# Pinned weight decodings, a sum of squares in two products, and one attention unit a step later

## The chip, the cores and the metric

The kernel runs on one core of a Trainium2 chip. The time is the device time of one execution in microseconds (us); the median of three runs before the change is 949.61 us (947.6 to 949.84). The core has four computing engines that matter here, each with its own instruction queue worked off in order: TensorE (PE; its weight loads are shown as PEld), VectorE (DVE), ScalarE (ACT) and GpSimd (POOL). SyncE (SP) issues the transfers. In an order or a timeline these short names stand.

## The reference

Three layers follow each other: a windowed attention with 32 global tokens per batch, a feed-forward layer with ELU, and a feed-forward layer with RMS normalisation and a SiLU gate. In short:

```python
x = attention(q_l, k_l, v_l, q_g, k_g, v_g)       # 4 batches, 8 heads, 512 + 32 rows, 64 wide
x = x.transpose(0, 2, 1, 3).reshape(2176, 512)    # 4 batches of 544 rows, 8 * 64 wide
h = x @ w_in                                      # 512 -> 2048
g = np.where(h > 0.0, h, np.exp(np.minimum(h, 0.0)) - 1.0)
x = g @ w_out                                     # 2048 -> 512
rms = np.sqrt(np.mean(x * x, axis=-1, keepdims=True) + 1e-06)
xn = x / rms * rms_g
g = xn @ w_gate                                   # 512 -> 1536
out = (g / (1.0 + np.exp(-g)) * (xn @ w_val)) @ w_out2  # 1536 -> 512
```

The weights arrive as 64-bit numbers; the rest as 32-bit.

## The kernel before, in words

**Number format.** Each 32-bit operand of the large products is kept as a high part and a low part in the reduced format fp32r, and a product is done in three passes (high by high, high by low, low by high; `PASSES`). Twelve such passes of 512 columns make one "first product" h (L128, 512 rows of weights deep) or one "second product" group y (L142).

**Weights.** A weight tile (two blocks of 128 rows by 512) is loaded as 64-bit words. Decoding it takes five steps and splitting two: ScalarE takes the absolute value of the upper word, read as a float (`dec_abs`, L79); VectorE clamps (L86), masks and shifts (L87) and merges in the bits of the two words (L88, L89); ScalarE casts the high part (L92); VectorE subtracts for the low part (L95). The feed-forward layer has 16 such tiles, numbered in the order `order1`: for each quarter G of the hidden width two tiles of w_in, then two of w_out. So tiles 0 and 1 are wanted from step 0 on, 2 from step 1 on, 8 and 9 by the first product of step 8, 12 and 13 by that of step 12.

**Stages.** A prologue computes the attention units 0 to 3 (a unit is 128 rows of one batch, all heads; units count from 0) and decodes tiles 0 to 2 in an order written by hand. Then four blocks of 512 rows follow (`moe_block`), each of 16 steps j. A step does the first product of step j (`mm1`), its activation (`act1`: on ScalarE L117, L118, on VectorE L119, then the split L135 on ScalarE and L136 on VectorE), and the second products of step j - 1 (`mm2`). During block b the attention units of the next batch are done in the gaps, one per four steps (`att_slot`): scores and exponentials at its first step (`a_S`, L211 to L221; `a_E`: maxima on VectorE L229, L230, eight exponentials on ScalarE L232), transposition at its second (`a_T`, L238, copied out by L240), value products and normalisation at its third (`a_PV`, L251; `a_N`, L264 to L266). In block 0 each step also ends with the decoding of one tile, 3 at step 0 to 15 at step 12 (`slot0`, `w1_decode`). The rest of the kernel (blocks 1 to 3, and the last layer in five groups of 512 or 384 rows, `prep` and the loop over k) uses the decoded weights; the last layer's weights are decoded during blocks 1 and 2, parked in HBM and fetched back through a small ring (`w2_fetch`). `prep` of a group has four parts: load, squares (L547, L553) added on GpSimd (L554), the sum over the 512 features by a product with a matrix of ones (L558) with root and reciprocal (L560, L561), and the scaled, split rows.

**What sets the order.** TensorE's order is the order of the code. On the other engines a scheduler moves instructions by its own estimate of when their inputs are there. Two things hold it: `tc.keep_in_program_order(ins)`, by which an instruction isn't moved ahead of the ones written before it, and `tc.issue_after(x)`, by which what is written inside comes after x. In block 0 the decodings stand under `issue_after` the last cast (`last[0]`, ScalarE) and the last subtraction (`last[1]`, VectorE) of the prologue's input.

Of the kernel before, what the change touches and what calls it, by code (L numbers as in the profile page):

```python
# [7 lines left out]
F32 = mybir.dt.float32  # L8
F32R = mybir.dt.float32r
# [3 lines left out]
ALU = mybir.AluOpType  # L13
# [17 lines left out]
def f(ap):  # L31
    return ap.bitcast(F32)
# [7 lines left out]
def fused_kernel(ctx: ExitStack, tc: tile.TileContext, kq, vl, gkq, gv, w_in, w_out, w_gate, w_val, w_o2, rms_g, consts, out):  # L40
# [36 lines left out]
    def dec_abs(pool, raw, keep=False):  # L77
        x = pool.tile([P, 1024], F32, tag="dx", name="dx")
        ins = nc.scalar.activation(x, f(words(raw)[:, :, 1]), AF.Abs)  # L79
        if keep:  # L80
            tc.keep_in_program_order(ins)
        return x
# [90 lines left out]
    with ExitStack() as ls:  # L173
# [107 lines left out]
        def att_slot(b, j, part):  # L281

            u, jj = 4 * (b + 1) + j // 4, j % 4
            if jj == 0 and part == 0:
                a_S(u, ATT2)
                a_E(u)
                load_kq(u + 1)
            if jj == 1 and part == 1:
                a_T(u, 0, aps, "att")
                a_T(u, 1, aps, "att")  # L290
            if jj == 2 and part == 0:
                a_PV(u, ATT2)
                a_N(u)
                load_v(u + 1)
# [55 lines left out]
        dxs, dsts = {}, {}  # L350

        def w1_abs(i):
            dxs[i] = dec_abs(dec["t"], raws[i])

        def w1_bits(i):
            dec_bits(dxs[i], raws.pop(i))
# [101 lines left out]
        def slot0(j, part, h):  # L458
            g = act1(h, 512, elu_a) if part == 0 else None
            att_slot(0, j, part)  # L460
            if part == 2:
                with tc.issue_after(last[0].ins), tc.issue_after(last[1].ins):
                    w1_decode()
                if j == 12:
                    w2_load()
                    w2_load()
            return g
# [24 lines left out]

    def second_start():
        bpools["bp"] = ctx.enter_context(tc.tile_pool(name="bp", bufs=1))
        bpools["ones"] = bpools["bp"].tile([P, P], F32, name="ones")
        nc.sync.dma_start(out=bpools["ones"], in_=consts[:, 4 * P:5 * P])
        bpools["gg"] = stage.enter_context(tc.tile_pool(name="ggp", bufs=2))
        bpools["st"] = stage.enter_context(tc.tile_pool(name="bst", bufs=4))
        prep(0, 0)
        w2_fetch()  # L500

    wraws, n_fetch = [], [0]

    def w2_fetch():
        while len(wraws) < 4 and n_fetch[0] < 18:
            raw = bpools["st"].tile([P, 1024], F32, tag="wraw", name="wraw")
            i = n_fetch[0]
            nc.sync.dma_start(out=raw.rearrange("p (a n) -> p a n", a=2), in_=wT[2 * i:2 * i + 2].rearrange("a p n -> p a n"))
            wraws.append(raw)
            n_fetch[0] += 1  # L510
# [24 lines left out]
    def prep(k, part):  # L535
        if k >= 5:
            return
        n = sizes[k] * P
        t0 = starts[k] * P
        if part == 0:  # L540
            y32 = moe.tile([P, 4, 512], F32, tag="x32", name="y32")
            nc.sync.dma_start(out=y32[:, :, :n], in_=yT[:, :, t0:t0 + n])
            y32_t[k] = y32
        elif part == 1:
            y32 = y32_t[k]
            acc = stg.tile([P, 512], F32, tag="stg", name="acc")
            nc.scalar.activation(acc[:, :n], y32[:, 0, :n], AF.Square)  # L547
            for c in range(1, 4):
                if k < 2:
                    sq = bpools["gg"].tile([P, 512], F32, tag="sq", name="sq")  # L550
                else:
                    sq = moe.tile([P, 512], F32, tag="e", name="sq", bufs=2)
                nc.scalar.activation(sq[:, :n], y32[:, c, :n], AF.Square)  # L553
                nc.gpsimd.tensor_tensor(out=acc[:, :n], in0=acc[:, :n], in1=sq[:, :n], op=ALU.add)  # L554
            acc_t[k] = acc
        elif part == 2:
            ms = hps.tile([P, 512], F32, tag="h", name="ms")
            nc.tensor.matmul(ms[:, :n], bpools["ones"], acc_t[k][:, :n], start=True, stop=True)  # L558
            rs = stg.tile([P, 512], F32, tag="stg", name="rs")
            nc.scalar.activation(rs[:, :n], ms[:, :n], AF.Sqrt, bias=eps, scale=1.0 / DM)  # L560
            nc.vector.reciprocal(rs[:, :n], rs[:, :n])  # L561
            rs_t[k] = rs
        else:
            y32, rs = y32_t[k], rs_t[k]
            if k % 2 == 0:
                xn = new_xT()
            else:
                xn = [bpools["xn"].tile([P, 2, 512], F32R, tag=f"xn{c}", name=f"xnB{c}") for c in range(4)]
            for c in range(4):
                nc.vector.scalar_tensor_tensor(out=y32[:, c, :n], in0=y32[:, c, :n], scalar=gcol[:, c:c + 1], in1=rs[:, :n], op0=ALU.mult, op1=ALU.mult)  # L570
                nc.scalar.copy(xn[c][:, 0, :n], y32[:, c, :n])
                nc.vector.tensor_tensor(out=xn[c][:, 1, :n], in0=y32[:, c, :n], in1=f(xn[c][:, 0, :n]), op=ALU.subtract)
            xn_t[k] = xn
# [337 lines left out]
```

## Time and profile before

| | us |
|---|---|
| median of 3 runs | 949.61 |
| the profiled execution | 949.2 |
| its span | 947.3 |
| TensorE busy | 915.8 (97%) |
| VectorE busy | 459.7 (49%) |
| ScalarE busy | 347.0 (37%) |
| GpSimd busy | 17.9 (2%) |

The share of a busy engine is a mean over the whole span: VectorE, at 49%, is busy without a gap in some stretches and nearly idle in others. In the page's 40 slices it stands at 9 in the third to fifth, which lie in block 0 of the first feed-forward layer; TensorE stands at 8 there and at 9 from the sixth on.

### The profile page before, as it was taken

What the parts mean: (1) busy time and instruction counts of PE and PEld (TensorE: products, weight loads), DVE (VectorE), ACT (ScalarE), POOL (GpSimd) and SP (SyncE); (2) the same over time, 40 slices, a digit from 0 to 9 for tenths busy, and PEclk for the clock granted to TensorE, in tenths of its full rate; (3) what the DMA queues carried; (4) which work ended last, traced back from release to release, by engine and by line L of the source; (5) the groups of instructions that cost most, each with busy time, mean ns of one, the idle gap of its engine ahead of it and who ended that gap; (6) DMA issues with size and microseconds to landing.
All of it is one profiled execution on the core that took longest, in us unless ns stands there. A gap on an engine that the chain in (4) does not pass through costs nothing.

```text
span 947.3 us, 15710 instructions
## 1 busy us (share of the span) xinstructions
PE 915.8 (97%) x6738; PEld 766.5 (81%) x6738; DVE 459.7 (49%) x791; ACT 347.0 (37%) x627; POOL 17.9 (2%) x19
## 2 busy tenths in 40 slices
PE   6788899999999999999999999999999999999997
PEld 5566688888887788777888888888889999999996
DVE  4799963666578874543786215221412241142111
ACT  4577544434443443332656213122312232232111
POOL 0000000000000000000100100001000100100000
PEclk9999999999999999999999999999999999999999
DMA  9675541544567763351644000100011010000000
GB/s 364 250 297 188 178 163 57 181 170 166 187 223 277 276 232 127 124 184 57 243 137 157 12 1 5 41 33 1 1 34 45 1 34 34 1 1 34 1 1 34
DMA packets 34445, 107.77 MB, mean 114 GB/s; under 512 B 3016, under 2 KB 5704, under 8 KB 31816
## 3 DMA queue, kind: packets, MB, share of 16 engines
q1 hardware_dynamic: 34376, 106.77, 31.5%
q8 instruction: 53, 0.87, 0.4%
q14 instruction: 16, 0.13, 0.0%
HBM read 88.41 MB, written 18.35 MB: 113 GB/s over the span
## 4 chain that ended last, share of the span: by engine, by line
PE 84%; DVE 8%; DMA 3%; issue 2%; ACT 2%; SPq 0%; ACTq 0%
PE y L142 15%; PE pg L633 15%; PE pv L633 15%; PE y L639 15%; PE h L128 14%; DVE dx L88 1%; DVE dx L89 1%; PE o L251 1%; PE yg L597 1%; PE s L221 1%; PE hg L581 1%; PE ptp L238 1%; DMA kq<-in_kq 1%; PE s L216 1%; DVE wA L95 1%
## 5 line engine op out<-in xcount | busy, mean ns | idle before, releaser
L142 PE MATMUL y<-g,wA 128*128 128x512 f32 x768 | 198.8, 402 | 6.1 <-DVE g L136 5.7
L128 PE MATMUL h<-xT,wA 128*128 128x512 f32 x768 | 186.8, 392 | 1.3 <-DVE xT L276 1.3
L142 PEld LDWEIGHTS y<-g,wA 128*128 128x128 f32 x768 | 140.2, 189 | 40.9 <-DVE g L136 8.4
L128 PEld LDWEIGHTS h<-xT,wA 128*128 128x128 f32 x768 | 144.2, 189 | 32.3 <-DVE xT L276 1.5
L806 DVE TENSOR_TENSOR silu<-pv,silu 128x384 f32<-128x384 f32 (+1 forms) x60 | 36.7, 611 | 257.2 <-PE pv L633 249.1
L639 PE MATMUL y<-wB,p 128*128 128x512 f32 x612 | 149.0, 391 | 0.0
L639 PEld LDWEIGHTS y<-wB,p 128*128 128x128 f32 x612 | 114.4, 188 | 22.3
L805 ACT ACTIVATE silu<-pg 128x384 f32<-128x384 f32 (+1 forms) x60 | 32.1, 534 | 158.9 <-PE pg L633 158.7
L633 PE MATMUL pv<-xT,wB 128*128 128x384 f32 (+1 forms) x432 | 88.4, 352 | 0.0
L633 PEld LDWEIGHTS pv<-xT,wB 128*128 128x128 f32 x432 | 77.3, 188 | 5.6
L808 ACT CAST p<-silu 128x384 fp32r<-128x384 f32 (+1 forms) x60 | 33.3, 555 | 127.0 <-DVE silu L806 126.8
L135 ACT CAST g<-e 128x512 fp32r<-128x512 f32 x64 | 39.8, 622 | 75.8 <-DVE e L111 71.0
L633 PE MATMUL pv<-xnB,wB 128*128 128x512 f32 (+1 forms) x288 | 61.5, 362 | 0.0
L109 ACT ACTIVATE e<-h 128x512 f32<-128x512 f32 x48 | 28.9, 601 | 85.3 <-PE h L128 77.9
L633 PE MATMUL pg<-xT,wB 128*128 128x384 f32 (+1 forms) x288 | 60.1, 357 | 0.0
L633 PEld LDWEIGHTS pg<-xT,wB 128*128 128x128 f32 x288 | 52.1, 188 | 5.8 <-issue 0.5
L633 PEld LDWEIGHTS pv<-xnB,wB 128*128 128x128 f32 x288 | 52.2, 188 | 5.6
L809 DVE TENSOR_TENSOR p<-silu,p 128x384 fp32r<-128x384 f32 (+1 forms) x60 | 38.0, 634 | 35.5 <-ACT p L808 35.5
L110 DVE TENSOR_SCALAR e<-e 128x512 f32<-128x512 f32 x52 | 22.2, 428 | 65.2 <-ACT e L109 65.0
L136 DVE TENSOR_TENSOR g<-e,g 128x512 fp32r<-128x512 f32 x64 | 45.1, 705 | 17.6 <-ACT g L135 16.3
L79 ACT ACTIVATE dx<-raw 128x1024 f32<-128x1024 f32 x34 | 39.5, 1162 | 10.9 <-DMA raw<-in_moe_w_out 4.3
L232 ACT ACTIVATE E<-s,mx 128x128 f32<-128x128 f32 x128 | 35.1, 384 | 22.3 <-DVE mx L230 22.3
(179 smaller groups left out, 948.5 us busy)
## 6 DMA issues: line engine op xcount, KB each, us to landing
raw<-in_moe_w_out SPq DMA_DIRECT2D x14, 1024.0 KB, 6.1
wT<-dx SPq DMA_DIRECT2D x18, 512.0 KB, 3.4
wraw<-wT SPq DMA_DIRECT2D x18, 512.0 KB, 4.2
raw<-in_moe_w_in SPq DMA_DIRECT2D x8, 1024.0 KB, 7.2
raw<-in_moe_w_gate SPq DMA_DIRECT2D x6, 1024.0 KB, 6.2
raw<-in_moe_w_val SPq DMA_DIRECT2D x6, 1024.0 KB, 6.8
gvr<-in_gv SPq DMA_DIRECT2D x8, 640.0 KB, 4.6
gkq<-in_gkq SPq DMA_DIRECT2D x4, 1152.0 KB, 5.2
```

What stands on the lines that cost most here:

```text
L79: ins = nc.scalar.activation(x, f(words(raw)[:, :, 1]), AF.Abs)
L128: nc.tensor.matmul(h[:, :n], W1[c, G][:, ws, o:o + P], xT[c][:, xs, :n], start=(k == 0), stop=(k == 11))
L135: nc.scalar.copy(g[:, 0, :n], e[:, :n])
L136: nc.vector.tensor_tensor(out=g[:, 1, :n], in0=e[:, :n], in1=f(g[:, 0, :n]), op=ALU.subtract)
L142: nc.tensor.matmul(ys[dc][:, :n], W2[j][:, ws, dc * P:(dc + 1) * P], g[:, gs, :n], start=(j == 0 and k == 0), stop=(j == 15 and k == 2))
L232: nc.scalar.activation(e[par][:, pr, :], ss[par][:, pr, :], AF.Exp, bias=mx[:, par, pr:pr + 1], scale=SCALE)
L633: nc.tensor.matmul(ps[:, :n], W[c, G3][:, ws, o:o + P], xn[c][:, xs, :n], start=(k == 0), stop=(k == 11))
L639: nc.tensor.matmul(os_[t], p[:, pp, t * P:(t + 1) * P], Wo[j][:, ww, :], start=(j == 0 and k == 0), stop=(j == 11 and k == 2))
L805: nc.scalar.activation(s[:, :n], pg[:, :n], AF.Silu)
L806: nc.vector.tensor_tensor(out=s[:, :n], in0=pv[:, :n], in1=s[:, :n], op=ALU.mult)
L808: nc.scalar.copy(p[:, 0, :n], s[:, :n])
L809: nc.vector.tensor_tensor(out=p[:, 1, :n], in0=s[:, :n], in1=f(p[:, 0, :n]), op=ALU.subtract)
```

## The change

It has three parts. In block 0 the absolute values of tiles 3 and up carry `keep`, so ScalarE's order has them where the code has them, at the end of a step; they no longer come after the prologue's last cast explicitly, only after the last subtraction. Unit 4, the fifth, has its scores, transposition and value products one step later (steps 1, 2 and 3 in place of 0, 1 and 2). In the last layer, the sums of squares are split into a high and a low part, and the product with ones is done twice in fp32r in place of once in 32 bits; the ones are written by GpSimd in place of being loaded, and the ring of fetched weights has three places in place of four, which makes the room.

```diff
@@ att_slot
             u, jj = 4 * (b + 1) + j // 4, j % 4
+            if b == 0 and j < 4:
+
+                jj = j - 1
             if jj == 0 and part == 0:
                 a_S(u, ATT2)
@@ w1_abs
-            dxs[i] = dec_abs(dec["t"], raws[i])
+            dxs[i] = dec_abs(dec["t"], raws[i], keep=i > 2)
@@ slot0
             if part == 2:
-                with tc.issue_after(last[0].ins), tc.issue_after(last[1].ins):
+                with tc.issue_after(last[1].ins):
                     w1_decode()
@@ second_start
-        bpools["ones"] = bpools["bp"].tile([P, P], F32, name="ones")
-        nc.sync.dma_start(out=bpools["ones"], in_=consts[:, 4 * P:5 * P])
+        bpools["ones"] = bpools["bp"].tile([P, P], F32R, name="ones")
+        nc.gpsimd.memset(f(bpools["ones"]), 1.0)
...
-        bpools["st"] = stage.enter_context(tc.tile_pool(name="bst", bufs=4))
+        bpools["st"] = stage.enter_context(tc.tile_pool(name="bst", bufs=3))
@@ w2_fetch
-        while len(wraws) < 4 and n_fetch[0] < 18:
+        while len(wraws) < 3 and n_fetch[0] < 18:
@@ prep, part 1
-            acc_t[k] = acc
+            a2 = bpools["bp"].tile([P, 2, 512], F32R, tag="a2", name="a2")
+            nc.scalar.copy(a2[:, 0, :n], acc[:, :n])
+            nc.vector.tensor_tensor(out=a2[:, 1, :n], in0=acc[:, :n], in1=f(a2[:, 0, :n]), op=ALU.subtract)
+            acc_t[k] = a2
@@ prep, part 2
-            nc.tensor.matmul(ms[:, :n], bpools["ones"], acc_t[k][:, :n], start=True, stop=True)
+            acc = acc_t[k]
+            for i in range(2):
+                nc.tensor.matmul(ms[:, :n], bpools["ones"], acc[:, i, :n], start=(i == 0), stop=(i == 1))
```

ScalarE, first steps of block 0, from the input's last cast on. Before (dx is the absolute value of a tile, wA its high part, E the exponentials of unit 4):

```order
L79 ACTIVATE dx<-raw 128x1024
L117 ACTIVATE e<-h 128x512
L118 ACTIVATE e<-e 128x512
L92 CAST wA<-dx 128x2x512
L135 CAST g<-e 128x512
L92 CAST wA<-dx 128x2x512
L117 ACTIVATE e<-h 128x512
L118 ACTIVATE e<-e 128x512
L79 ACTIVATE dx<-raw 128x1024
L232 ACTIVATE E<-s,mx 128x128 x8
L135 CAST g<-e 128x512
```

The same place after the change:

```order
L117 ACTIVATE e<-h 128x512
L118 ACTIVATE e<-e 128x512
L92 CAST wA<-dx 128x2x512
L135 CAST g<-e 128x512
L79 ACTIVATE dx<-raw 128x1024
L117 ACTIVATE e<-h 128x512
L118 ACTIVATE e<-e 128x512
L135 CAST g<-e 128x512
L92 CAST wA<-dx 128x2x512
L232 ACTIVATE E<-s,mx 128x128 x8
L79 ACTIVATE dx<-raw 128x1024
L117 ACTIVATE e<-h 128x512
```

The absolute value of tile 3 moved from ahead of step 0's activation to behind it, that of tile 4 from ahead of the exponentials to behind them, and the high part of tile 3 from between the steps to behind step 1's activation.

ScalarE, around the exponentials of unit 5 (step 4). Before; the two absolute values are those of tiles 8 and 9:

```order
L79 ACTIVATE dx<-raw 128x1024
L92 CAST wA<-dx 128x2x512
L135 CAST g<-e 128x512
L79 ACTIVATE dx<-raw 128x1024
L232 ACTIVATE E<-s,mx 128x128 x8
L92 CAST wA<-dx 128x2x512
L117 ACTIVATE e<-h 128x512
```

After the change; the absolute values are those of tiles 7 and 8:

```order
L135 CAST g<-e 128x512
L232 ACTIVATE E<-s,mx 128x128 x8
L79 ACTIVATE dx<-raw 128x1024
L117 ACTIVATE e<-h 128x512
L118 ACTIVATE e<-e 128x512
L92 CAST wA<-dx 128x2x512
L240 COPY ET<-ptp 128x512
L135 CAST g<-e 128x512
L240 COPY ET<-ptp 128x512
L79 ACTIVATE dx<-raw 128x1024
```

Two absolute values stood ahead of the exponentials; now the next one, of an earlier tile, stands behind them.

VectorE, from the second maximum of unit 5 on. Before (tiles 8 and 9 are under way):

```order
L230 TENSOR_SCALAR mx<-mx 128x4
L87 TENSOR_SCALAR dx<-dx 128x1024
L89 SCALAR_TENSOR_TENSOR dx<-raw,dx 128x1024
L88 SCALAR_TENSOR_TENSOR dx<-raw,dx 128x1024
L95 TENSOR_TENSOR wA<-dx,wA 128x2x512
L89 SCALAR_TENSOR_TENSOR dx<-raw,dx 128x1024
L119 SCALAR_TENSOR_TENSOR e<-e,h 128x512
```

After the change (tile 7 follows, alone):

```order
L230 TENSOR_SCALAR mx<-mx 128x4 x2
L86 TENSOR_SCALAR dx<-dx 128x1024
L87 TENSOR_SCALAR dx<-dx 128x1024
L88 SCALAR_TENSOR_TENSOR dx<-raw,dx 128x1024
L89 SCALAR_TENSOR_TENSOR dx<-raw,dx 128x1024
L119 SCALAR_TENSOR_TENSOR e<-e,h 128x512
L95 TENSOR_TENSOR wA<-dx,wA 128x2x512
```

Two tiles were interleaved there; now one tile's steps follow each other, and the first of them is the one that needs the absolute value behind the exponentials.

## Rows read from the trace of the kernel before

**Rows 1.** The page: the span, and TensorE's busy time, share, instructions.

```profile
span 947.3 us, 15710 instructions
...
PE 915.8 (97%) x6738; PEld 766.5 (81%) x6738; DVE 459.7 (49%) x791; ACT 347.0 (37%) x627; POOL 17.9 (2%) x19
```

**Rows 2.** Waits of TensorE, 42 to 165 us: total, times, longest.

```profile
PE y L142 <- DVE g L136: 5.3, 4, 2.5
```

**Rows 3.** Busy time by stretch: us, PE, PEld, DVE, ACT, POOL, clock, DMA.

```profile
42.60:119.50 76.90, 67.94 (x623) 53.41 (x624) 76.66 (x107) 50.77 (x83) 0.00 (x0) 0.98 0.57 207
54.50:57.90 3.40, 3.40 (x13) 2.51 (x12) 3.33 (x6) 3.40 (x10) 0.00 (x0) 0.50 1.02 423
```

**Rows 4.** Timeline of TensorE, block 0: start, us, engine, line, what.

```profile
42.63 3.01 PE L128 MATMUL h<-xT,wA 128*128 128x512 f32 x12 [1.29 <-DVE xT L276]
...
45.48 0.61 PE L211 MATMUL s<-masks,identr 128*128 128x512 f32 x2
...
47.97 3.00 PE L128 MATMUL h<-xT,wA 128*128 128x512 f32 x12
...
102.95 2.88 PE L128 MATMUL h<-xT,wA 128*128 128x512 f32 x12
...
134.02 2.88 PE L128 MATMUL h<-xT,wA 128*128 128x512 f32 x12
...
146.15 1.03 PE L238 MATMUL ptp<-ident,E 128*128 128x128 f32 x8
...
151.21 1.12 PE L251 MATMUL o<-v__1454,ET 128*32 128x65 f32 x64
...
162.33 2.88 PE L128 MATMUL h<-xT,wA 128*128 128x512 f32 x12
```

**Rows 5.** Timeline of VectorE, block 0.

```profile
56.16 0.69 DVE L87 TENSOR_SCALAR dx<-dx 128x1024 int32<-128x1024 int32 x1
56.89 1.23 DVE L88 SCALAR_TENSOR_TENSOR dx<-raw,dx 128x1024 int32<-128x1024 int32 x1
58.03 0.69 DVE L136 TENSOR_TENSOR g<-e,g 128x512 fp32r<-128x512 f32 x1
58.64 0.69 DVE L86 TENSOR_SCALAR dx<-dx 128x1024 f32<-128x1024 f32 x1
...
90.89 1.22 DVE L95 TENSOR_TENSOR wA<-dx,wA 128x1024 fp32r<-128x1024 f32 x1
...
116.02 1.22 DVE L95 TENSOR_TENSOR wA<-dx,wA 128x1024 fp32r<-128x1024 f32 x1
```

**Rows 6.** Timeline of ScalarE, block 0.

```profile
54.13 2.16 ACT L232 ACTIVATE E<-s,mx 128x128 f32<-128x128 f32 x8
...
79.58 1.15 ACT L79 ACTIVATE dx<-raw 128x1024 f32<-128x1024 f32 x1 [0.78 <-DVE wA L95]
```

**Rows 7.** Timeline of TensorE, last layer, around two sums of squares.

```profile
573.56 2.88 PE L633 MATMUL pv<-xT,wB 128*128 128x512 f32 x12
576.28 2.88 PE L639 MATMUL y<-wB,p 128*128 128x512 f32 x12
...
582.63 0.62 PE L633 MATMUL pv<-xT,wB 128*128 128x512 f32 x2
...
753.56 2.24 PE L639 MATMUL y<-wB,p 128*128 128x512 f32 x9
...
757.75 2.24 PE L633 MATMUL pv<-xT,wB 128*128 128x384 f32 x12
759.83 2.24 PE L639 MATMUL y<-wB,p 128*128 128x512 f32 x9
...
764.64 1.55 PE L633 MATMUL pv<-xT,wB 128*128 128x384 f32 x8
```

**Rows 8.** Timeline of ScalarE and GpSimd after the fifth group's squares.

```profile
827.44 0.49 ACT L805 ACTIVATE silu<-pg 128x384 f32<-128x384 f32 x1 [1.99 <-PE pg L633]
...
825.53 1.01 POOL L554 TENSOR_TENSOR acc<-acc,sq 128x384 f32<-128x384 f32 x1 [0.64 <-ACT sq L553]
```

## The prediction

> **What bounds the kernel now.** I read the page first: TensorE is busy for 97% of the span [rows 1]. So only what shortens its work, or a wait of its own, can show. The waits of TensorE, asked for the first block of the mixture (42 to 165 us), come second: its largest is for the activated tile g, 5.3 us in four waits, the longest 2.5 [rows 2]. After that block TensorE waits for nearly nothing until the output is stored. Third, the busy time of each engine by stretch: from 42.6 to 119.5 us VectorE works 76.66 of 76.90 us [rows 3]. In that block it, not TensorE, is the engine without slack: it must decode and split twelve weight tiles (2 to 13; 14 and 15 follow) beside the activations. The timelines then give the price of each instruction and the four marks that I use, the starts of the block's first products of steps 0, 8, 12 and, for the next block, 16: 42.63, 102.95, 134.02 and 162.33 us [rows 4].
>
> **The pinned decodings and the later scores.** Price on VectorE, from one start to the next [rows 5]: the two clamps and masks of a tile 0.60 us each (0.73 when the next one needs the result, that is 0.12 more), the two bit merges and the low part 1.13 each, so 4.59 us for a tile; the two instructions of an activated tile 0.60 each. An attention unit adds some 2.35 (two reductions at 0.60, eight small ones). Four steps with four tiles and one unit make 4 x 4.59 + 4 x 1.20 + 2.35 = 25.5 us, and the trace agrees: the low parts of tiles 9 and 13 start 25.1 us apart [rows 5].
>
> In the old order ScalarE takes the absolute value of tile 9 at 79.58 us, ahead of the exponentials of unit 5 [rows 6], and the tile is split at 92.1 us, over 12 us before step 8 multiplies by its second half. That lead keeps VectorE fed. The second and third of the pieces in the section on the change show what the pin does: behind the unit's eight exponentials now stands the absolute value of tile 7, not two tiles ahead of them. I laid both orders out by hand, each instruction at the later of its engine being free and its inputs being there, with the durations of these rows. For the old order that gives 119.2 us from mark 0 to mark 16, where the trace has 119.7, so the method is good to about 0.5 us. For the new order:
>
> - Steps 0 and 1 gain. The scores of unit 4 (units count from 0) no longer stand between the first two products, tile 3 is no longer interleaved with tile 2, and the longest wait for g [rows 2] goes.
> - What is late next is step 2's own g. ScalarE's high part of tile 3 stands in front of the exponentials and of step 2's activation and waits 3.6 us for VectorE; TensorE then waits 4.6 us ahead of step 2's second products. At step 4 the two orders are level within 0.4 us.
> - VectorE now idles, where it was full. After the maxima of unit 5 it waits for eight exponentials (2.0 to 2.2 us [rows 6]) and then the absolute value (1.15 us): 3.2 us. Up to tile 9 I count seven more such gaps of 0.6 to 1.9 us, all behind a pinned absolute value or a high part queued on ScalarE: 10.2 us in all. Its work to that point is 8 tiles x 4.59 + 16 x 0.60 + 2 units x 2.35 + the first 1.2 of tile 10 = 52.2 us, and some 14 results needed at once cost 14 x 0.12 = 1.7. So tile 9 is split at 43.1 + 52.2 + 10.2 + 1.7 = 107.2 us.
> - TensorE wants it after 8.5 first products and 7 second ones of 2.72 us, two scores of 2.49 (45.48 to 47.97), two sets of transposes and two value products (1.03 and 1.12 each in the rows, of which some 0.15 lies under the next: 3.7 together) and 8.8 us of laid-out waits: 42.6 + 42.2 + 5.0 + 3.7 + 8.8 = 102.3 us [rows 4]. It stands 4.9 us. The old order passes this point at 102.95 + 1.36 = 104.3, so the new one is 2.9 us late.
> - The next four steps repeat it. VectorE needs 25.5 + 9 x 0.12 + gaps of 3.2, 0.6, 0.8 and 0.6 = 31.8 us against 31.07 between the marks [rows 4]: tile 13 holds step 12 for another 4.8 us, and the delay is 3.6.
> - From there the old order needs 26.95 us to mark 16, the new one 26.4 of work and 1.8 of waits (step 14's value products wait for a copy queued behind tile 15's high part on ScalarE): 1.2 more. Delay at the end of the block: 4.8 us. Nothing behind the block gives it back, since TensorE is busy without a gap there.
>
> **The clock.** After the 2.5 us wait the granted clock is 0.50 (1.2 of 2.4 GHz) from 54.5 to 57.9 us [rows 3], and once more late in the block; the half clock costs TensorE up to 3.4 / 2 = 1.7 us each time. The new order has three waits of about 4.8 us (steps 2, 8, 12), longer than those. I take one fall more than before, and two thirds of its price since VectorE is the late one after some of them: 1.1 us. Bounds: 0 and 3 x 1.7 = 5.1.
>
> **The sum of squares.** Per unit of the last stage the 32-bit product stands between two groups. From the second products to the next value products TensorE takes 582.63 - 576.28 = 6.35 us with it and 5.44 without (two groups of 2.72, as 573.56 to 576.28): 0.91 us. For 384 columns it is 4.81 against 4.19: 0.62 [rows 7]. Two full-rate products are 2 x 0.227 and 2 x 0.18. The gain is 2 x 0.46 + 3 x 0.26 = 1.7 us, and TensorE has no slack there, so all of it counts. The nearest rows bound it: nothing if a product of the new form took 0.48 us like a half of the old one, 1.7 if it runs like its neighbours; I take 1.7. The two added splits per unit are hidden: the third sum on GpSimd ends at 826.54, the cast of 0.5 us is done by 827.1, and ScalarE waits for pg until 827.44 in any case [rows 8]. Without that cover each would cost at most the 1.0 us by which it would hold ScalarE, five times. Fetch buffers (three for four), the ones written by GpSimd instead of a transfer and the fewer transfers on SyncE I set at nothing, between -0.5 and +1.0 together: no product of that stage waits for its weights. The raw load of tile 11 now queues behind a value load on SyncE until step 5 has multiplied; it lands some 18 us ahead of its use in my layout.
>
> **Sum.** 4.8 + 1.1 - 1.7 = +4.2 us. The profiled execution took 949.2 us (span 947.3), 0.4 below the median of 949.61; on the median the change gives 953.8 us.
>
> A rule that would make the first stall larger: the Trainium skill, VectorE: DVE Perf Modes, "The DRAIN you can't avoid", says that a Vector instruction starts only once the pipe of the one before it is empty, whatever the semaphores. By it the step between bit merges would be their 1.23 us, and tile 9 would come some 4 us later still. The row has the next one 0.09 us before that end (56.89 + 1.23 against 58.03 [rows 5]), so I use 1.13.
>
> **The rivals.**
> - *The clock falls after each of the three long waits and TensorE is then the late engine.* Place: steps 2, 8 and 12. Price 5.1 in place of 1.1: 949.6 + 8.2 = 957.8 us. For it: the fall at 54.5 followed a wait of half that length. Against: where VectorE is late anyway, a slow TensorE costs nothing; after the first fall the old order lost little. The Trainium skill, TensorE: Matmul & The Clock Gate, "HAM oscillation — how this bites in real kernels", has idle gaps between groups of products lower the clock, which is this rival; the stretch at 0.50 agrees.
> - *The pins work as worded.* The activations of the first steps come sooner, and tiles 9 and 13 are there in time. It decides if VectorE's gaps stay under some 5 us up to tile 9. Then four fifths of the 5.3 us [rows 2] go, with the 1.7 of the squares: 949.6 - 4.2 - 1.7 = 943.7, faster. For it: the longest wait does go. Against: the 3.2 us behind the exponentials, which no other work on VectorE's order fills.
> - *It cancels out.* The stalls at tiles 9 and 13 are real but half as long (a gap or two filled earlier than I laid it), 1.5 to 2 us, and the squares pay for them: 949.6 us.
> - *The split of the squares does not gain*, because the cast waits for GpSimd and holds the Silu behind it: then 955.5. The covers above speak against it; it lies in the range.
>
> **How the numbers follow.** Under 0.3%, 2.8 us here, a measurement can't tell a change from none. Forecast 0.64, with its own range 951.5 to 956.5; of it 0.06 lies within 0.3%. Clock rival 0.14. Cancelling out 0.15. Faster rival 0.07. So slower 0.58 + 0.14 = 0.72, same 0.15 + 0.06 = 0.21, faster 0.07. The range 948.5 to 957.5 leaves out most of the faster rival (0.06), half of the clock one (0.07) and little else.
>
> **What would show it.** Right: two new waits of TensorE of about 4.8 us inside the first products of steps 8 and 12, put down to the low part of a weight tile on VectorE; idle time of VectorE for the absolute value, 3.2 us after each unit's maxima; the last low part of the block near 155 us instead of 128; 0.45 us instead of 0.91 for each sum of squares. Wrong: first products of steps 8 and 12 without a wait, mark 16 less than 2 us later than 119.7 after mark 0, or a new wait in the last stage.

## The result, and the profile after

The changed kernel takes 956.68 us (median of 4 runs, 955.62 to 959.74) against 949.12 (median of 4, 947.6 to 949.84). The ratio is 1.0087, with a 95% interval of 1.0058 to 1.0116: slower by 7.6 us, where 4.2 on top of the median of 949.61, 953.8 us in all, was forecast. The profiled execution took 957.72 us. The page answers [rows 1]: the span is 8.6 us longer, and TensorE is busy 2.7 us longer for the same number of instructions.

```profile
span 955.9 us, 15715 instructions
...
PE 918.5 (96%) x6738; PEld 770.4 (81%) x6738; DVE 466.4 (49%) x796; ACT 348.7 (36%) x632; POOL 18.6 (2%) x20
```

The waits of TensorE in the first block, 42 to 172 us (total, times, longest), answer [rows 2]. The wait for g has shrunk from 5.3 us to 2.4 and 1.8; in its place stand 6.7 and 1.4 us for a weight tile, wA.

```profile
PE h L128 <- ACT wA L92: 6.7, 2, 3.4
PE y L142 <- DVE g L136: 2.4, 1, 2.4
PE y L142 <- ACT g L135: 1.8, 1, 1.8
PE h L128 <- DVE wA L95: 1.4, 2, 0.9
```

TensorE's timeline (start, us, line, what, idle time before it and its releaser) answers [rows 4] and shows the places: in front of the second products of step 2's g (which stand in step 3), and inside the first products of steps 8 and 12.

```profile
67.76 0.50 PE L142 MATMUL y<-g,wA 128*128 128x512 f32 x1 [1.76 <-ACT g L135]
70.61 4.86 PE L142 MATMUL y<-g,wA 128*128 128x512 f32 x11 [2.36 <-DVE g L136]
...
102.47 1.52 PE L128 MATMUL h<-xT,wA 128*128 128x512 f32 x6
107.33 0.73 PE L128 MATMUL h<-xT,wA 128*128 128x512 f32 x2 [3.34 <-ACT wA L92]
108.99 1.90 PE L128 MATMUL h<-xT,wA 128*128 128x512 f32 x4 [0.93 <-DVE wA L95]
...
135.37 1.52 PE L128 MATMUL h<-xT,wA 128*128 128x512 f32 x6
140.24 1.22 PE L128 MATMUL h<-xT,wA 128*128 128x512 f32 x2 [3.35 <-ACT wA L92]
141.90 2.08 PE L128 MATMUL h<-xT,wA 128*128 128x512 f32 x4 [0.44 <-DVE wA L95]
```

The busy time by stretch (us; then PE, PEld, DVE, ACT, POOL; granted clock; DMA) answers [rows 3]: first the whole block (mark 0 is 43.65, mark 16, the first product of the next block, 170.96), then the three stretches at or near half clock, each behind one of those waits. The second fence has the same block of the kernel before and the second fall of its clock, which [rows 3] do not show.

```profile
43.65:170.96 127.31, 114.14 (x1005) 90.13 (x1005) 100.36 (x147) 69.81 (x119) 0.00 (x0) 0.93 0.46 164
68.30:75.10 6.80, 4.49 (x11) 3.52 (x12) 6.80 (x12) 2.19 (x2) 0.00 (x0) 0.50 1.01 415
109.20:112.80 3.60, 3.60 (x70) 2.54 (x69) 2.67 (x3) 1.84 (x3) 0.00 (x0) 0.53 0.07 15
139.97:146.80 6.83, 6.12 (x78) 4.09 (x80) 5.45 (x7) 2.90 (x5) 0.00 (x0) 0.50 0.57 192
```

```profile
42.63:162.33 119.70, 110.78 (x1004) 88.48 (x1005) 97.62 (x147) 70.82 (x119) 0.00 (x0) 0.97 0.49 175
119.30:122.70 3.40, 3.40 (x9) 2.65 (x9) 2.96 (x5) 3.14 (x5) 0.00 (x0) 0.51 0.52 142
```

The block is 127.31 - 119.70 = 7.61 us longer: 114.14 - 110.78 = 3.36 of it is TensorE working longer on the same products, and the other 4.25 is TensorE standing. The 3.36 is clock: half of the work at half clock is 7.1 us in this block (4.49, 3.60 and 6.12 us) and 3.4 in the block before (twice 3.40). The split says what TensorE did, not what either part would have cost without the other. On VectorE (answer to [rows 5]) the eight exponentials and the absolute value leave 3.19 us empty behind unit 5's maxima; the low part of tile 9 starts at 107.71 (before at 90.89), that of the block's last tile at 157.71 (before at 128.20). On ScalarE ([rows 6]) the absolute value stands where the order shown ahead of the prediction puts it.

```profile
83.34 0.29 DVE L230 TENSOR_SCALAR mx<-mx 128x4 f32<-128x4 f32 x2
86.81 0.70 DVE L86 TENSOR_SCALAR dx<-dx 128x1024 f32<-128x1024 f32 x1 [3.19 <-ACT dx L79]
...
107.71 1.22 DVE L95 TENSOR_TENSOR wA<-dx,wA 128x1024 fp32r<-128x1024 f32 x1
...
157.71 1.23 DVE L95 TENSOR_TENSOR wA<-dx,wA 128x1024 fp32r<-128x1024 f32 x1 [1.12 <-ACT wA L92]
```

```profile
83.59 2.18 ACT L232 ACTIVATE E<-s,mx 128x128 f32<-128x128 f32 x8 [2.09 <-PE y L142]
85.61 1.17 ACT L79 ACTIVATE dx<-raw 128x1024 f32<-128x1024 f32 x1
```

In the last layer (TensorE, answer to [rows 7]) a sum of squares now costs 589.44 - 588.99 = 0.45 us at 512 columns and 771.46 - 771.11 = 0.35 at 384. On ScalarE and GpSimd (answer to [rows 8]) the fifth group's cast is over at 836.01, and the Silu waits for pg as before.

```profile
588.99 0.62 PE L566 MATMUL ms<-a,ones 128*128 128x512 f32 x2
589.44 2.88 PE L641 MATMUL pg<-xT,wB 128*128 128x512 f32 x12
```

```profile
835.50 0.51 ACT L559 CAST a<-acc 128x384 fp32r<-128x384 f32 x1 [1.12 <-POOL acc L557]
836.36 0.49 ACT L813 ACTIVATE silu<-pg 128x384 f32<-128x384 f32 x1 [0.35 <-PE pg L641]
```

Three marks on TensorE split the rest: mark 16, the first gx, a transposition of the gathered rows (403.88 us before, 413.75 after), and the end of the last product (940.70 and 949.34).

| stretch | before | after | difference |
|---|---|---|---|
| span's start to mark 0 | 42.63 | 43.65 | +1.02 |
| block 0 (mark 0 to 16) | 119.70 | 127.31 | +7.61 |
| mark 16 to first gx | 241.55 | 242.79 | +1.24 |
| first gx to last product | 536.82 | 535.59 | -1.23 |
| rest of the span | 6.60 | 6.56 | -0.04 |

The first line differs from execution to execution: in the profiles of the other kernels below mark 0 lies between 41.87 and 43.69, with the same instructions of TensorE and VectorE in front of it. The other four sum to 7.58 us, near the 7.56 between the two medians. One of the twelve executions of the kernel below that keeps tile 3's place only took 3183.74 us; the ratio leaves it out.

### The profile page after: what moved, and what is told of

It is laid out like the page before. It is cut to its first block, busy times and chain, and to the rows that moved or that the text cites. A ratio compares the mean times of both kernels' runs of the same rounds, so it can differ in the third digit from the quotient of the medians.

```text
span 955.9 us, 15715 instructions
## 1 busy us (share of the span) xinstructions
PE 918.5 (96%) x6738; PEld 770.4 (81%) x6738; DVE 466.4 (49%) x796; ACT 348.7 (36%) x632; POOL 18.6 (2%) x20
## 4 chain that ended last, share of the span: by engine, by line
PE 80%; DVE 10%; ACT 5%; DMA 2%; issue 2%; SPq 0%; ACTq 0%; DVEq 0%
PE pg L641 15%; PE pv L641 15%; PE y L647 15%; PE y L142 14%; PE h L128 13%; DVE dx L88 2%; DVE dx L89 2%; PE o L251 1%; DMA kq<-in_kq 1%; PE s L221 1%; ACT E L232 1%; DVE g L136 1%; PE s L216 1%; PE ptp L238 1%; DVE dx L86 1%
## 5 line engine op out<-in xcount | busy, mean ns | idle before, releaser
L88 DVE SCALAR_TENSOR_TENSOR dx<-raw,dx 128x1024 int32<-128x1024 int32 x34 | 42.1, 1239 | 0.9
```

The lines of the kernel that those rows point to most:

```text
L88: nc.vector.scalar_tensor_tensor(out=i32(x), in0=word[:, :, 1], scalar=-0x40000000, in1=i32(x), op0=ALU.bitwise_and, op1=ALU.bitwise_or)
```

## The experiments

All kernels below were timed in five rounds; the kernel before had medians of 948.71, 948.70 and 948.85 us beside the three sets of four. "Block 0" is mark 0 to mark 16 of the profiled execution.

### Which edit costs

Theory A was the prediction's: the kept places starve VectorE. B was that the later scores do the harm, C that the squares do. The edits, in this order: `keep` alone; the later scores alone; the squares alone; and the changed kernel without `keep`.

```diff
# e_pin: the kernel before, with
+            dxs[i] = dec_abs(dec["t"], raws[i], keep=i > 2)
# e_shift: the kernel before, with
+            if b == 0 and j < 4:
+                jj = j - 1
# e_squares: the kernel before, with the new prep part 1 and 2, ones by memset, ring of three
# e_nopin: the changed kernel, with
-            dxs[i] = dec_abs(dec["t"], raws[i], keep=i > 2)
+            dxs[i] = dec_abs(dec["t"], raws[i])
```

> The kernel before with one of the three edits alone: absolute values of weight tiles 3 to 15 kept at their place in ScalarE's order; no later scores, old squares. Theory A (the kept places starve VectorE of weight tiles, TensorE then waits for a low part, and its clock falls behind the waits): +3.5 us from the waits by a hand lay-out of the new order, and 0 to 5 more from the clock, so 953 to 958, with two new waits inside first products of the first block put down to a low part of a weight tile. Theory B (the later scores of unit 4 cause the loss, since they put exponentials in front of tile work): within 1 us of before, no such waits. Theory C (the new squares cost more than they save): within 1 us of before.

> The kernel before with the later scores alone: unit 4's scores, transposes and value products one step later in the first block, no kept places, old squares. Theory A: no loss, -0.5 us by the lay-out (-2 to +1), no wait for a weight tile in the first block. Theory B: +4 to +8 us, with the wait in front of the second products of step 2 and the clock fall behind it as in the changed kernel. Theory C: within 1 us of before.

> The kernel before with the squares alone: high and low part of the accumulated squares multiplied by ones at the full rate, ones written on chip, three buffers for the second half's weights instead of four. The first block stays as it was. Theory A: -1.7 us (0.46 saved twice and 0.26 three times by the rows of the two kernels), 946.9 to 948.3. Theory C: the added copy and subtraction, or the ring of three, cost more than the 1.7 us: 0 to +3 us, with new TensorE waits after 480 us. Theory B says nothing here.

> The changed kernel with the kept places alone taken out again: later scores and new squares stay. Theory A: faster than before, -1 to -4 us by the lay-out (the later scores and the squares both gain), the waits for low parts of weight tiles gone from the first block. Theory B: still +4 to +6 us, the wait in front of step 2's second products still there. Theory C: still slower than before by +2 or more, the loss behind 480 us.

| kernel | median, us | ratio to before, 95% | block 0 |
|---|---|---|---|
| kept places alone | 955.50 | 1.0070 [1.0055, 1.0085] | 125.57 |
| later scores alone | 949.45 | 1.0005 [0.9996, 1.0014] | 119.39 |
| squares alone | 947.89 | 0.9989 [0.9977, 1.0000] | 120.36 |
| changed, without kept places | 948.55 | 0.9993 [0.9982, 1.0005] | 119.47 |

The kept places alone bring 6.8 of the 7.6 us, and without them nothing is left of the loss. B and C fall. The order behind the prologue's last cast, which the change drops, costs nothing that shows: the last kernel drops it too, and its order in block 0 is that of the kernel with the later scores alone; only one absolute value stands elsewhere, just ahead of mark 0. The two waits for wA are there in the first kernel (its waits of TensorE, first fence) and its granted clock over the block is 0.92 (second fence, by stretch); in the other three they are absent.

```profile
PE h L128 <- ACT wA L92: 4.6, 2, 3.2
```

```profile
43.69:169.26 125.57, 114.87 (x1004) 91.52 (x1005) 99.83 (x147) 70.03 (x119) 0.00 (x0) 0.92 0.47 167
```

A's gain for the kernel without kept places (-1 to -4) was a miss: -0.2 us, within the measurement. Its block 0 gains 0.23, its last layer 1.46 us, and 0.64 goes at the start of block 2, by a wait that is taken up below. The squares alone were to bring 1.7 and bring 0.8. Their profile shows where a part goes: ScalarE waits 2.99 us for a fetched weight tile in front of the first root, the reciprocal behind it starts late, VectorE then works without a gap, and a transposition on TensorE waits 0.82 us for it (ScalarE's and TensorE's timelines).

```profile
486.08 1.05 ACT L92 CAST wB<-wraw 128x1024 fp32r<-128x1024 f32 x1 [2.99 <-DMA wraw<-wT]
```

```profile
500.59 0.63 PE L593 MATMUL egt<-ident,e 128*128 128x128 f32 x4 [0.82 <-DVE e L111]
```

### Is it the place behind the exponentials?

If VectorE starves because the kept absolute value stands behind a unit's exponentials, it is enough to issue it a step earlier, with every place still kept. One kernel does that, one keeps tile 3's place only.

```diff
# e_abs_early: the changed kernel, with
-                w1_abs(i)
+                if i not in dxs:
+                    w1_abs(i)
...
                 w1_load()
+                if i + 1 < 16:
+                    w1_abs(i + 1)
# e_pin_to3: the changed kernel, with keep=2 < i <= 3
```

> The changed kernel with one thing moved: the absolute value of the next weight tile is issued at the end of the step before, so that on ScalarE it stands ahead of a unit's eight exponentials instead of behind them; all places stay kept. Theory A (VectorE starves because the kept absolute value stands behind the exponentials): VectorE's idle stretches of 2 to 3 us behind a unit's maxima go, the waits for a low part inside steps 8 and 12 go, and block 0 is no longer than before's 119.7 us; the lay-out makes it 112 to 114, so 942 to 949 us in all. Theory D (a kept order as such costs, wherever the absolute value stands, since ScalarE can no longer pick what is ready): still 953 to 957 us, with waits of the same size elsewhere.

> The changed kernel with one kept place only, that of weight tile 3 in step 0; tiles 4 to 15 float. Theory A (what costs is the kept place behind a unit's exponentials, and tile 3 has none ahead of it): no loss, 945.5 to 949 us, no wait for a low part at steps 8 and 12, block 0 within 119.7 -2.5 to +0.5. Theory D (any kept place costs in proportion to their number): a tenth of the loss, within 1 us of the kernel without kept places, 948.5. If tile 3's place alone shifts the whole chain late: +2 us or more.

Measured: 941.62 us, ratio 0.9922 [0.9909, 0.9935], for the first, 947.24 us, ratio 0.9981 [0.9968, 0.9994], for the second. D falls, A stands. In the first kernel ScalarE takes the absolute value at 77.56, ahead of the exponentials at 79.67 (first fence), and VectorE goes from unit 5's maxima to the next tile without a gap (second fence), where the changed kernel had 3.19 us. Block 0 is 113.48 us, at a granted clock of 1.00 (third fence).

```profile
77.56 1.13 ACT L79 ACTIVATE dx<-raw 128x1024 f32<-128x1024 f32 x1
79.67 2.18 ACT L232 ACTIVATE E<-s,mx 128x128 f32<-128x128 f32 x8 [0.98 <-DVE mx L230]
```

```profile
79.41 0.23 DVE L230 TENSOR_SCALAR mx<-mx 128x4 f32<-128x4 f32 x2
79.55 0.69 DVE L86 TENSOR_SCALAR dx<-dx 128x1024 f32<-128x1024 f32 x1
```

```profile
42.38:155.86 113.48, 107.75 (x1005) 86.12 (x1006) 100.10 (x147) 70.39 (x119) 0.00 (x0) 1.00 0.51 184
```

That is 7.1 us faster than the kernel before. Two more kernels asked which edits this gain needs: the same without the later scores (and with the old squares), and the same with the places free.

```diff
# e_early_noshift: e_pin, with the absolute value one step ahead
# e_early_float: e_abs_early, without keep
```

> The kernel before with kept places and the absolute value one step ahead, but without the later scores of unit 4 and with the old squares. If the earlier absolute value alone makes the gain of 7 us: 941.5 to 944 us. If it only undoes what the kept places cost (the lay-out: block 0 +0.1 to +0.5) and the gain needs the later scores as well: 948 to 950 us, 5 to 7 below the kernel with kept places alone.

> The kernel that was 7 us faster, without the kept places: the absolute value of the next tile is written one step ahead, but its place on ScalarE is left to the scheduler. If the kept place is what holds it ahead of the exponentials (theory A): the gain goes for the most part, 946 to 949 us, near the changed kernel without kept places. If writing it earlier is enough: 941 to 943 us.

Measured: 951.89 us, 1.0035 [1.0021, 1.0048], and 947.84 us, 0.9989 [0.9980, 0.9998]. So the gain needs all three: kept, early, and the later scores (the old squares of the first kernel are worth 2.0 us at most, by the stretches below). In the second kernel the order of ScalarE and VectorE in block 0 is, instruction by instruction, that of the changed kernel without kept places: where the scheduler was free, it undid the earlier writing. The first kernel gains 3.6 us over the kept places alone, less than the 5 to 7 expected, and stays slower than before. Its rows show the same fault at another place. Without the later scores unit 4's exponentials fall into step 0 and stand ahead of even the early absolute value (ScalarE); VectorE waits 3.19 us for it, and TensorE 4.21 us for a tile at step 4.

```profile
51.28 2.17 ACT L232 ACTIVATE E<-s,mx 128x128 f32<-128x128 f32 x8 [2.71 <-DVE mx L230]
53.29 1.18 ACT L79 ACTIVATE dx<-raw 128x1024 f32<-128x1024 f32 x1
```

```profile
54.50 0.69 DVE L86 TENSOR_SCALAR dx<-dx 128x1024 f32<-128x1024 f32 x1 [3.19 <-ACT dx L79]
```

```profile
74.48 3.33 PE L128 MATMUL h<-xT,wA 128*128 128x512 f32 x6 [4.21 <-ACT wA L92]
```

### What the clock costs

The next kernel was to put products that nobody reads in front of the waiting ones, so that TensorE does not stand. They write a spare bank of the scores. At steps 8 and 12 they stand where the waits are; those of step 2 stand in front of the second products of step 1's g, a step ahead of the waits for step 2's. A second one does it to the kernel before, at the two waits behind which its clock fell.

```diff
# e_fill: the changed kernel; filler(place) issues the number of products given for that place
+    fill = {step 2: 7 and 10, step 8: 14 and 4, step 12: 14 and 2}
+            for _ in range(m):
+                nc.tensor.matmul(t, W1[0, 0][:, 0, 0:P], junk["x"][0][:, 0, :], start=True, stop=True)
# e_fill_before: the kernel before; 10 such products into ys[3] at step 1, 7 and 4 into pt at step 9
```

> The changed kernel with products that nobody reads put in front of the products that wait (17 at step 2, 18 at step 8, 16 at step 12, about 0.24 us each), so that TensorE stays busy through the waits while every order stays as it is; the clock should then not fall. If the clock falls are a term of their own, as the 6.8 us at half clock behind the last wait suggest (3.4 us of work lost there): granted clock 1.00 behind steps 2, 8 and 12, block 0 at 123 to 125 us instead of 127.3, 952.5 to 955 in all. If the waits alone make the loss (the lost clock is caught up in the next wait): block 0 at 126.5 to 129, 956 to 959.

> The kernel before with products that nobody reads put in front of the two waits behind which its clock falls in the first block (10 at the 2.5 us wait of step 1, 11 at the two waits of 1.6 and 0.9 us of step 9). If the two falls of 3.4 us each cost TensorE half of their length (3.4 us in all): no fall to half clock, the filling products aside TensorE's busy time of block 0 falls from 110.8 to about 107.4 us, block 0 from 119.7 to 116 to 118, 945 to 947.5 us in all. If a lost clock is given back by shorter waits later: block 0 stays at 119.7 and the time at 948.7, and the waits of steps 5, 6 and 9 get longer by what was saved.

The filled kernel takes 949.63 us, 1.0013 [1.0004, 1.0022]: with 51 added products it is 7.0 us faster than the changed kernel, where 1.7 to 4.2 were expected. By stretch (first fence), block 0 is 121.82 us at clock 1.00, 5.5 less than without them. At step 8 TensorE's timeline (second fence) has the 14 fillers and then no wait at all: the high part of tile 9 is there, and its low part starts at 104.20 on VectorE (third fence).

```profile
42.34:164.16 121.82, 118.11 (x1055) 95.80 (x1056) 99.40 (x147) 70.53 (x119) 0.00 (x0) 1.00 0.48 172
```

```profile
101.04 3.33 PE L131 MATMUL junk<-xT,wA 128*128 128x512 f32 x14
104.21 0.62 PE L140 MATMUL h<-xT,wA 128*128 128x512 f32 x2
```

```profile
104.20 1.22 DVE L95 TENSOR_TENSOR wA<-dx,wA 128x1024 fp32r<-128x1024 f32 x1
```

The clock is not the only thing that the fillers changed, though. The expectation counted on every order staying as it is; on ScalarE and VectorE the scheduler moved instructions from step 2 on. The fillers of step 2 wait 1.73 us themselves, for exponentials that still read the bank they write (TensorE, first fence below). And ScalarE takes tile 8's absolute value ahead of tile 7's high part (second fence), in the changed kernel behind it (third fence).

```profile
57.84 1.88 PE L131 MATMUL junk<-xT,wA 128*128 128x512 f32 x7 [1.73 <-ACT E L245]
```

```profile
87.97 1.15 ACT L79 ACTIVATE dx<-raw 128x1024 f32<-128x1024 f32 x1
89.83 1.06 ACT L92 CAST wA<-dx 128x1024 fp32r<-128x1024 f32 x1 [0.72 <-DVE dx L89]
```

```profile
90.79 1.05 ACT L92 CAST wA<-dx 128x1024 fp32r<-128x1024 f32 x1 [2.86 <-DVE dx L89]
...
93.22 1.25 ACT L79 ACTIVATE dx<-raw 128x1024 f32<-128x1024 f32 x1
```

Measured from mark 0, the low part of tile 9 starts at 104.20 - 42.34 = 61.86 us with the fillers and at 107.71 - 43.65 = 64.06 without, 2.2 us later. The fall behind step 2 is not seen to do that: VectorE takes up tile 7 at 43.05 us with the fillers and at 43.16 without, level, and from that fall to tile 9 VectorE waits for ScalarE alone, and ScalarE for VectorE but once (2.1 us for TensorE, ahead of exponentials whose maxima come no earlier). Of the 2.2 us, 1.3 are two of these waits (0.52 and 0.81 us, at tiles 7 and 8), which the other order of ScalarE does not have. So the 7.0 us are the falls and the orders together, and how they divide this kernel does not show.

One fall can be priced from the changed kernel's own rows. Around and behind step 12's wait TensorE does 6.12 us of work at half clock, 3.06 of them lost, and no wait follows this fall in the block. From where step 12 goes on (140.24 us without fillers, 136.51 with) to mark 16 it takes 30.72 us without and 27.65 with, 3.1 less. The remaining gains of the filled kernel over the changed one's profile lie behind the block (0.5 us to the first gx, 0.75 in the last layer, where the wait at the transposes is absent) and in the varying start.

The filled kernel before takes 950.39 us, 1.0016 [1.0007, 1.0025]: slower by 1.5 us, where 945 to 947.5 was expected if lost clock counts in full. Its clock is 1.00 over the block, which is 119.77 us long, as was expected if lost clock is given back. (The 1.5 us lie behind the block: from mark 16 to the first gx it takes 242.94 us, 1.4 more than before, with the wait in block 2 that is taken up below.) The fillers of step 1 replace the wait of 2.5 us by one of 0.23, but step 2's wait for VectorE's g grows from 0.41 to 1.27 us, and step 4 starts 29.29 us after mark 0 where it was 29.21, with ScalarE's and VectorE's order unchanged up to there. There the lost clock had been given back. The fillers of step 9 tell less: the bank they write was still being read by the exponentials, so they stood behind the wait of 1.60 us that they were to fill.

```profile
41.91:161.68 119.77, 112.55 (x1026) 90.11 (x1026) 97.63 (x147) 70.70 (x119) 0.00 (x0) 1.00 0.49 175
```

### The squares' ring, and the two together

> The kernel before with the new squares, and the second half's weight ring left at four buffers (the two parts of the sum lie in buffers that the squares had anyway). If the ring of three takes back part of the 1.7 us (ScalarE waited 3.0 us for a weight tile just before the first sum, and TensorE 0.4 to 0.8 us at the transposes behind it): -1.7 us, no such wait, the stretch from the first gx product to the end 535.0 to 535.3 us against 536.8 of before. If the squares themselves gain less than their rows: about -1.0 as with the ring of three, 535.8 us.

> The kernel that was 7 us faster, with the second half's weight ring at four buffers as in the run on the squares. By that run's median nothing is gained over the ring of three (947.87 against 947.89): 941 to 942 us. If the ring's wait of 0.4 to 0.8 us at the transposes goes without another taking its place: 940.5 to 941.2 us.

```diff
# e_sq4: e_squares with the ring of four; high and low part in the buffers of the squares
-            a2 = bpools["bp"].tile([P, 2, 512], F32R, tag="a2", name="a2")
+            if k < 2:
+                hi, lo = [bpools["gg"].tile([P, 512], F32R, tag="sq", name="hl") for _ in range(2)]
+            else:
+                hl = bpools["xn"].tile([P, 2, 512], F32R, tag="a2", name="a2")
+                hi, lo = hl[:, 0], hl[:, 1]
...
# e_best: e_abs_early with the same edit
```

Measured: 947.87 us, 0.9989 [0.9979, 0.9999], and 942.50 us, 0.9932 [0.9921, 0.9944]. The ring of four takes away ScalarE's wait in front of the first root, but the time is that of the ring of three (947.87 against 947.89), and the second kernel is no faster than the one with the ring of three (942.50 against 941.62); a gain of 0.4 us, as the expectation had it, is less than these medians tell apart. From the first gx to the last product it takes 535.43 and 535.44 us, 1.4 less than before, with a wait of 0.32 us on VectorE in front of the product behind the first sum. Three kernels with the ring of three and no such wait (the early, the filled and the one with tile 3 alone kept) take 534.84, 534.84 and 534.81: 2.0 less than before.

What tells them from the others with a ring of three is how long ScalarE waits for the fetched tile. It is 1.45 to 1.51 us in these three. In the other four (the changed kernel, the squares alone, the changed kernel without kept places, the early one with free places) it is 2.72, 2.99, 2.52 and 2.92, and the transposes wait 0.60, 0.82, 0.40 and 0.80 for VectorE: what exceeds some 2.1 us reaches TensorE. So a ring of three costs where the tile comes late. Why it comes at different times was not tried.

## Why the prediction was right, and where its sizes were off

The direction held, the time lies in the range, at its upper end. Term by term, against the prediction's working:

**The place and the cause held.** VectorE's gap behind unit 5's maxima was put at 3.2 us and is 3.19; tile 9 was laid out to be split by 107.2 and is, with mark 0 moved back by 1.02, by 107.71 + 1.22 - 1.02 = 107.9, with 9.7 us of VectorE's waits up to there where gaps of 10.2 were laid out; the last low part was to come near 155 and starts at 156.7 on the same scale. The waits were laid out as 4.6 us at step 2, 4.9 at step 8 and 4.8 at step 12; they are 1.76 + 2.36 = 4.1, 3.34 + 0.93 = 4.3 and 3.35 + 0.44 = 3.8. The prediction put the last two down to the low part on VectorE. The rows name the high part on ScalarE for most of them; for tile 9 that cast starts at 106.24 us, 0.46 after VectorE's last bit merge ends (105.78), so the late engine is the one named, an instruction earlier. The early absolute value, with every place still kept, took most of these waits with it: TensorE waits 2.0 us for weight tiles in its block 0, in the changed kernel 8.1.

**The sum of the waits, +4.8, was near: +4.25.** The 1.8 us laid out at step 14 did not come (between step 14 and mark 16 the new order takes 0.35 us more). The way there was another, too: the delay was laid out as 2.9 us behind step 8's wait and 3.6 behind step 12's, and the starts of steps 9, 12 and 13, counted from mark 0, are 4.8, 0.3 and 7.3 us late. The old order loses at step 9 by its own waits (1.64 and 0.86 us) and its second fall what the new one lost at step 8, and so nearly all of the net loss comes from the last of the three places.

**The step that failed is the clock, +1.1.** It is +3.36. The prediction had one fall more than before and two thirds of 1.7 us, since VectorE would be late anyway. There are three falls, two of them 6.8 us long, where before had two of 3.4. And the discount held only in the old order: there a fall is given back for the most part (the filled kernel before; and the kernels with the squares alone, last section). In the new order the fall behind step 12 has no wait after it to give it back: 3.1 us. The clock rival named the three places and the mechanism, and had 5.1 us for it. Its argument against itself, that a slow TensorE costs nothing where VectorE is late, does not reach that last place; for the falls behind steps 2 and 8, which waits follow, no run here separates their cost from that of the orders. The Trainium skill, TensorE: Matmul & The Clock Gate, section "HAM oscillation — how this bites in real kernels", puts such falls down to gaps between groups of products; the fillers agree (0.93 before them, 1.00 with them).

**The squares, -1.7, gave -1.2.** The five sums save what was said (0.45 us each at 512 columns where 0.91 was read, 0.35 at 384 against 0.62). The stretch from the first gx to the end gets up to 2.0 us shorter in kernels where nothing waits; in the changed kernel 0.60 us goes at the second half's transposes (TensorE's timeline), a wait that was not foreseen, that comes by way of ScalarE's 2.72 us for a fetched tile and the late reciprocal, and that the prediction's cover for the fetch buffers ("no product of that stage waits for its weights") did not look at, since what waits there is a transposition, for VectorE.

```profile
509.05 0.63 PE L596 MATMUL egt<-ident,e 128*128 128x128 f32 x4 [0.60 <-DVE e L111]
```

**The small things, 0, gave +1.2.** In step 2 of block 2, in front of the second products of step 1's g (TensorE's timeline), a wait of 1.35 us and the slow products behind it are new. This wait, 0.8 to 1.4 us, is in the changed kernel and in nine of the twelve others, but not in the kernel before, with the kept places alone, or in the two with the squares alone. It comes even where nothing but filling products was added. ScalarE's timelines tell the kernels apart: in all ten with the wait one copy of block 1's result (L155) stands ahead of the exponentials, in the four without it both stand behind (before at 280.99, behind exponentials at 278.92; after at 285.14, ahead of those at 287.27), and ScalarE waits 3.3 to 4.6 us in place of 1.7 to 2.7 for the storing of that result before it takes up step 1's exponential. So it goes with a new order that the scheduler chose there; that order alone was not tried.

```profile
298.98 0.50 PE L142 MATMUL y<-g,wA 128*128 128x512 f32 x1 [1.35 <-ACT g L135]
```

Together 4.25 + 3.36 + 1.24 - 1.23 = 7.6 us, against 4.8 + 1.1 - 1.7 = 4.2.

**The other rivals.** That the pins work as worded needed VectorE's gaps under some 5 us; it took the early absolute value to get there (4.3 us up to tile 9), and then the time is 941.6, near the 943.7 that this rival gave. Cancelling out fell with the waits of 4 us. That the squares do not gain fell with the rows above.

## What to carry to other kernels

Pinning an instruction fixes what stands in front of it too: look at what the engine does just ahead of the pinned place, and issue the pinned work before that, not after it. Where an engine without slack feeds TensorE, a wait costs its own length and, behind it, the clock; the second part is given back only where a later wait can absorb it, so price the last wait of a stage with the half of the half-clock stretch that is lost behind it. A kernel with products that nobody reads in front of the waits is a clean test of the clock only if the scheduler left the other engines' orders as they were: compare those before reading its time.

## What the runs showed of the hardware

The same wait does not always bring a fall. In the profiled execution of the squares with the ring of four, whose block 0 has the old order (instruction by instruction on ScalarE and VectorE), TensorE waits 2.50 us at step 1 as in [rows 2], and the clock over the next 3.4 us is 1.00 where [rows 3] have 0.50 (by stretch, first fence). TensorE is busy 1.6 us less than before in that block, stands 1.8 us longer, and the block is as long: 119.90 against 119.70 us. The squares with the ring of three have the same order there too, and their execution went the other way (second fence): the granted clock is 0.96, TensorE is busy 1.2 us longer than before, and the block takes 0.66 us more. So with one order over three executions, 2.75 us of TensorE's work between the fastest and the slowest make 0.46 us of time. Over the whole kernel a lower clock does go with a longer time: of the 81 executions of the kernel before beside the experiments, the 27 with a mean granted clock of 0.991 or less have a median of 949.7 us, the 23 with 0.995 or more 948.3.

```profile
42.73:162.63 119.90, 109.22 (x1005) 87.35 (x1005) 97.67 (x147) 70.67 (x119) 0.00 (x0) 0.99 0.49 175
54.60:58.00 3.40, 2.85 (x16) 2.00 (x15) 3.33 (x6) 3.40 (x10) 0.00 (x0) 1.00 1.03 424
```

```profile
43.31:163.67 120.36, 111.97 (x1004) 89.99 (x1005) 97.61 (x147) 70.67 (x119) 0.00 (x0) 0.96 0.49 174
```

Why a fall comes in one execution and not in the next, no run here shows. Products that nobody reads kept the clock up: 51 of them, 51 x 0.227 = 11.6 us of work, took the granted clock of block 0 from 0.93 to 1.00, and the kernel, with the orders that came with them, was 7 us faster for all that work; 21 in the kernel before took it from 0.97 to 1.00 and gained nothing.
